# Sliding-window attention in front of a mixture of experts: exponentials by block and head, with the maximum as bias and the row sum as second output

## Chip, cores and metric

One core of one Trainium2 chip runs the whole program. The metric is the time of the device from start to end in microseconds (us), as the median of several executions. Its engines are named as in the profile: PE (matrix multiplication), PEld (PE's weight loads), DVE (the vector engine), ACT (the scalar engine), POOL (GpSimd) and SP (which issues most DMAs).

## The reference

Four batches of 768 tokens, eight heads of 64. Each token attends to the last 128 tokens and to the first four ("sinks"). The result, 3072 rows of 512, goes through a layer of eight experts, of which each token takes two. Of the attention:

```python
scores = scale * np.matmul(q, k.transpose(0, 1, 3, 2))
keep = is_sink | in_window
scores = np.where(keep, scores, -1000000000.0)
scores = scores - np.max(scores, axis=-1, keepdims=True)
a = np.exp(scores)
a = a / (np.sum(a, axis=-1, keepdims=True) + 1e-09)
return np.matmul(a, v).astype(np.float32)
```

The experts follow (noisy gate, best two of eight, two matrix products with a ReLU between, weighted sum). Everything is float32; q and k are scaled so that the scores spread widely.

## The kernel before, in words

**Stages.** The program has an attention stage and an expert stage. In the attention stage the routing of each finished batch is mixed in; the routing of the last batch falls into the expert stage. The change touches the attention stage alone.

**Tiles.** A unit of work `n` (48 in all) is one pair of heads and two neighbouring blocks of 128 queries: four pairs of block and head, `u` = 0 to 3. For each `u` there are 128 rows with `KW` = 132 columns: four for the sinks and 128 for one key per distance. Since a query of a block sees a triangle of its own block and the opposite triangle of the block before, the two triangles fit together into 128 columns. The tile `C(n)` is thus 128 x 4 x 132, in a ring of five (`cbuf`).

**The steps of one unit**, with engine and line: `qk` (PE, L314) makes scores of the previous and the own block in PSUM tile `S`; `prev` (ACT, L317) copies the previous block's with the sinks into `C`; `cur` (DVE, L322 or L324) writes the own block's triangle over it; `cur1` (DVE, L331) masks a few sink columns of a pair of heads' first unit; `mins` (DVE, L334) takes the maximum of each row and `u`, four numbers `mn`; `sub` (POOL, L337, which the profile shows as L221, the line of the helper `minus`) subtracts it; `exps` (ACT, L341) is one exponential over 528 columns with the scale 1/8; `sums` (DVE, L344) adds up each row and `u` over 133 columns, of which the last always holds 1e-9; `sums_i` (DVE, L352) takes the reciprocal. `pcopy` (ACT L363 or POOL L361) and `plow` (POOL, L221 again) split the sink columns into a high and a low part in `pcbuf`. `ptr` (PE, L372) transposes the 128 columns of each `u` into PSUM tile `P`, `ptr_c` (ACT, L375) copies it to `CT`, `ptr_m` (POOL L384 or DVE L382) masks it into `CM`; `pv` (PE, L389 to L398) multiplies by the values and by the differences `dv` of neighbouring value blocks; `sink_c` (ACT, L402), `sinks` (PE, L407), `pv_c` (ACT, L415), `rows` (PE, L420) and `rows_c` (DVE, L423, times the reciprocal) finish the unit, and `rows_d` (SP) writes it out. The line numbers of the changed kernel are one higher from L345 on.

**What sets the order.** Every step is given to a planner (`Plan.op`) with its engine, a booked duration, a priority and the buffers it reads and writes. `Plan.run` walks through time with these durations, takes on each engine the ready step with the lowest priority number, and then emits the instructions in the order of the planned starts. Each engine runs its instructions in exactly that order. The priorities are the unit's number plus a constant from the table `PR` (`exps`, `exps_0` for the first two pairs of heads, `exps_9` for the last two, and so on); `pc_pool` says for how many units in eight `pcopy` goes to POOL. Rings bound how far a unit can run ahead: five of `C`, three of `mn`, four of `sm`, two of `S`, one of `P`, three of `X` (the results in PSUM).

Of the kernel before, what the change touches and what calls it, by code (L numbers as in the profile page):

```python
# [9 lines left out]
F32 = mybir.dt.float32  # L10
# [6 lines left out]
AF = mybir.ActivationFunctionType  # L17
OP = mybir.AluOpType
AX = mybir.AxisListType
BIG = 1.0e30  # L20
PR = dict(dv_pool=3, cm_pool=11, gap=1.5, pc_pool=2, warm=1, cur=0.024, cur1=1.512, cur1_0=-2.463, cur1_9=-0.944,
          cur_0=-2.879, cur_9=7.138, dv=-0.208, dv_0=3.364, dv_9=-0.999, exps=-275.071, exps_0=0.236, exps_9=-12.521,
          ga=217.688, gt=32.64, lg=-2.337, load_qk=1.266, load_v=-14.107, mins=31.945,
          mins_0=-4.24, mins_9=-2.207, nosink=-1.301, nosink_0=-0.047, nosink_9=-0.253, pcopy=6.03, pcopy_0=1.686,
          pcopy_9=7.368, plow=13.607, plow_0=0.131, plow_9=0.771, prev=0.291, prev_0=1.379, prev_9=51.746, ptr=0.719,
          ptr_0=-28.087, ptr_9=2.286, ptr_c=0.721, ptr_c_0=-1.706, ptr_c_9=0.124, ptr_m=1.76, ptr_m_0=1.659,
          ptr_m_9=-7.049, pv=5.174, pv_0=-10.632, pv_9=-9.441, pv_c=0.422, pv_c_0=-1035.731, pv_c_9=-0.357,
          qk=-18.348, qk_0=-9.938, qk_9=1.363, rows=3.058, rows_0=-0.428, rows_9=0.074, rows_c=-3.885,
          rows_c_0=-741.395, rows_c_9=2.644, rt=3.336, sink_c=-35.588, sink_c_0=7.46, sink_c_9=-0.144, sinks=-3.864,
          sinks_0=-0.51, sinks_9=-0.67, sub=15.081, sub_0=14.492, sub_9=19.966, sums=560.828, sums_0=1.201,  # L30
          sums_9=14.127, sums_i=27.946, sums_i_0=-7.208, sums_i_9=-17.917, w1=19.111,
          stay=49.741)
CAP = 832
COLD = 6.0
KQ, PB, XB = 3, 1, 3
FIRST = 4
ZEROS = 16

# [5 lines left out]
class Plan:  # L44
# [16 lines left out]
    def get(self, tag, i, shape=None, dt=F32, pool="sb", pad=None):  # L61
        kx = (tag, i)
        if kx not in self.live:
            more = {"padded_shape": pad} if pad else {}
            self.live[kx] = self.pools[pool].tile(shape, dt, name=tag, bufs=self.rings[tag], **more)
        return self.live[kx]
# [153 lines left out]
def minus(eng, out, a, b):  # L220
    eng.tensor_tensor(out, a, b, op=OP.subtract)  # L221


def attention(tc, plan, consts, cst, sh, qk_t, v, vsink, xbuf):
    nc = tc.nc
    H, S, D, NB, NS, XW = sh.H, sh.S, sh.D, sh.NB, sh.NS, sh.XW
    HP = H // 2
    NJ = NB // 2
    KW = 128 + NS
    NP = sh.B * HP  # L230
    plan.rings.update(vr=2, vn=2, dv=2, skn=2, sqn=2, kq=KQ, C=5, mn=3, sm=4, ri=2, pc=3,
                      CT=2, CM=2, ps=3, xr=3, S=2, P=PB, X=XB, xtn=5, lt=1, lm=1, lg=2)
    get, op = plan.get, plan.op
    jp, idf, idr = cst["jp"], cst["idf"], cst["idr"]
# [7 lines left out]
    nc.vector.tensor_copy(m1, m0[:, :NS])  # L242
    nc.vector.memset(m0[:, :NS], 0.0)

    cbuf = consts.tile([128, plan.rings["C"], 4, KW + 1], F32, name="cbuf")
    nc.gpsimd.memset(cbuf[:, :, :, KW:], 1e-9)

    pcbuf = consts.tile([128, plan.rings["pc"], 128], F32R, name="pcbuf")
    nc.gpsimd.memset(pcbuf.bitcast(F32), 0.0)
# [5 lines left out]
    vst = [plan.next("st") for _ in range(sh.B)]  # L255

    def C(n):
        return cbuf[:, n % plan.rings["C"], :, :KW]

    def vs(b):  # L260
        return get("st", vst[b], [128, 1024], F32, "early").rearrange("p (a g h d) -> p a g h d", a=2, h=2, d=D)
# [71 lines left out]
    def mins(n):  # L333
        nc.vector.tensor_reduce(get("mn", n, [128, 4]), C(n), op=OP.max, axis=AX.X)  # L334

    def sub(n, eng):
        minus(nc.gpsimd if eng == "Pool" else nc.vector, C(n), C(n),  # L337
              get("mn", n)[:, :, None].to_broadcast([128, 4, KW]))

    def exps(n):  # L340
        nc.scalar.activation(C(n), C(n), AF.Exp, scale=1.0 / math.sqrt(D))  # L341

    def sums(n):
        nc.vector.tensor_reduce(get("sm", n, [128, 4]), cbuf[:, n % plan.rings["C"]], op=OP.add, axis=AX.X)  # L344

    def rib(n):
        g, jj = divmod(n, NJ)
# [85 lines left out]
    def P(g, nm):  # L433
        return PR.get(nm, 0) + (PR.get(nm + "_0", 0) if g < 2 else PR.get(nm + "_9", 0) if g >= NP - 2 else 0)

# [6 lines left out]
    def loads_v(g):  # L442
        plan.dma((g - 1) * NJ + PR.get("load_v", 1), lambda: load_v(g), 1.9, w=[("vn", g)])

# [7 lines left out]
    for g in range(NP):  # L452
        p0 = g * NJ
        e = p0 - NJ
        if g:
            load(g, None, (g - 3) * NJ + PR.get("load_qk", 0) if g > 1 else -1980)
            loads_v(g)
        else:
            plan.dma(-1998, lambda: load_v(0), 1.9, w=[("vn", 0)])
        if g % HP == 0:  # L460
            b, z = g // HP, (g - HP) * NJ if g else -6
            plan.dma(z if g else -1996, lambda b=b: sink_values(b), 2.2, w=[("st", vst[b])])
            z += 9 if g else 0
            op("ACT", .95, z, lambda b=b: sink_hi(b), r=[("st", vst[b])], w=[("vr", b)])
            op("DVE", 1.2, z, lambda b=b: sink_lo(b), r=[("st", vst[b])], w=[("vr", b)])
        de = "Pool" if g % 4 < PR.get("dv_pool", 4) else "DVE"
        op(de, 1.5 if de == "Pool" else .74, p0 + .5 + P(g, "dv"), lambda g=g, de=de: dv(g, de), r=[("vn", g)], w=[("dv", g)])
        for jj in range(NJ):
            n = p0 + jj
            if not jj:  # L470
                op("Pool", .05, n + P(g, "nosink"), lambda n=n: nosink(n), w=[("C", n, 0)], u=[("C", n)])
            for a in range(2):
                z = n + .2 * a
                s = 2 * n + a
                need = {max(jj - 1, 0), jj} if not a else {jj}
                op("PE", .5 if jj or a else .3, z + P(g, "qk"), lambda n=n, a=a: qk(n, a),
                   r=[("kq", g, i) for i in sorted(need)], w=[("S", s)], u=[("kq", g)], kind=1)
                if jj or a:
                    op("ACT", .27, z + P(g, "prev"), lambda n=n, a=a: prev(n, a), r=[("S", s)], w=[("C", n, a)], u=[("C", n)])
                op("DVE", .335, z + P(g, "cur"), lambda n=n, a=a: cur(n, a), r=[("S", s)], w=[("C", n, a)], u=[("C", n)])  # L480
            if not jj:
                op("DVE", .085, n + .4 + P(g, "cur1"), lambda n=n: cur1(n), w=[("C", n, 1)], u=[("C", n)])
            op("DVE", .62, n + .4 + P(g, "mins"), lambda n=n: mins(n), r=[("C", n, 0), ("C", n, 1)], w=[("mn", n)], u=[("C", n)])
            op("Pool", 1.03, n + .4 + P(g, "sub"), lambda n=n: sub(n, "Pool"), r=[("mn", n)], w=[("C", n)])
            op("ACT", .53, n + .4 + P(g, "exps"), lambda n=n: exps(n), w=[("C", n)])
            pe = "Pool" if n % 8 < PR.get("pc_pool", 0) else "ACT"
            op(pe, .12 if pe == "ACT" else .23, n + .5 + P(g, "pcopy"), lambda n=n, pe=pe: pcopy(n, pe), r=[("C", n)], w=[("pc", n)])
            op("Pool", .18, n + .5 + P(g, "plow"), lambda n=n: plow(n), r=[("C", n)], w=[("pc", n)])
            op("DVE", .62, n + .8 + P(g, "sums"), lambda n=n: sums(n), r=[("C", n)], w=[("sm", n)])
            op("DVE", .094, n + .6 + P(g, "sums_i"), lambda n=n: sums_i(n), r=[("sm", n)], w=[("rin", n)], u=[("ri", g // HP)])  # L490
            op("PE", .43, n + .5 + P(g, "ptr"), lambda n=n: ptr(n), r=[("C", n)], w=[("P", n + NJ)])
            op("ACT", .48, n + .5 + P(g, "ptr_c"), lambda n=n: ptr_c(n), r=[("P", n + NJ)], w=[("CT", n)])
            me = "Pool" if n % 12 < PR.get("cm_pool", 0) else "DVE"
            op(me, (.6 if jj else .33) * (1 if me == "DVE" else .98), n + .5 + P(g, "ptr_m"), lambda n=n, me=me: ptr_m(n, me),
               r=[("P", n + NJ) if me == "DVE" else ("CT", n)], w=[("CM", n)])
            XA[n] = xa = plan.next("X")
            op("PE", 1.12 if jj else .9, n + .6 + P(g, "pv"), lambda n=n: pv(n),
               r=[("vn", g), ("CT", n), ("dv", g), ("CM", n), ("pc", n)], w=[("X", xa)], kind=2)
            op("ACT", .17, n + .6 + P(g, "sink_c"), lambda n=n: sink_c(n), r=[("X", xa)], w=[("ps", n)])
            op("PE", .24, n + .6 + P(g, "sinks"), lambda n=n: sinks(n), r=[("ps", n), ("vr", g // HP)], w=[("X", xa)], kind=3)  # L500
            op("ACT", .27, n + .6 + P(g, "pv_c"), lambda n=n: pv_c(n), r=[("X", xa)], w=[("xt", n)], u=[("xtn", g)])
            op("PE", .22, n + .7 + P(g, "rows"), lambda n=n: rows(n), r=[("xt", n)], w=[("X", xa)], u=[("xtn", g)])
            op("DVE", .34, n + .7 + P(g, "rows_c"), lambda n=n: rows_c(n), r=[("X", xa), ("rin", n)], w=[("xr", n)],
               u=[("ri", g // HP)])
            plan.dma(n + .7, lambda n=n: rows_d(n), .37, r=[("xr", n)], w=[("xrow", n)])
            yield n
# [770 lines left out]
```

## Time and profile before

| | |
|---|---|
| median of 3 executions | 819.08 us (818.0 to 819.09) |
| the profiled execution | 817.08 us, with a span of 815.5 us from the first to the last instruction |
| busy in the span | PE 777.9 us, PEld 651.9, DVE 437.1, ACT 320.6, POOL 428.2 |
| attention stage | about 8 to 195 us |
| expert stage | about 195 to 815 us |
| mean granted PE clock | 0.985 |

A row of the windows view gives the stretch, its length, then busy time and number of instructions of PE, PEld, DVE, ACT and POOL, the granted PE clock, the share of the DMA engines and GB/s; with a source line it counts that line's instructions alone. A row of the groups view names line, engine, operation, output and input with their shapes and the count; behind the bar stand the busy time and the mean time of one in ns, then the idle time of the engine before them and what ended it. A row of the timeline has start, length, engine, line and operation, and in brackets the idle time before it. A row of the source view has the count and the shortest, median and longest time in ns.

### The profile page before, as it was taken

Reading aid. Unit: us, or ns where it says so; the run is one execution under the profiler, and the core shown is the slowest. Engines: PE = TensorE matmul, PEld = TensorE weight load, DVE = VectorE, ACT = ScalarE, POOL = GpSimd, SP = SyncE. Lnnn points to the kernel's source line nnn. Section 1 sums busy time; section 2 is a strip of 40 time slices with the busy share of each in tenths; the row PEclk is TensorE's granted clock in tenths of the full one; section 3 lists DMA queues with packets and bytes.
Section 4 is the critical chain, followed back from the end, with each engine's and each line's share of the span. In section 5 each row is a group of like instructions: output and inputs, shape, how many; then the busy total and the mean of one; then the engine's idle time right before and its main releaser. Section 6 shows DMA issues by size and latency. Waiting matters only on the chain.

```text
span 815.5 us, 12512 instructions
## 1 busy us (share of the span) xinstructions
PE 777.9 (95%) x4609; PEld 651.9 (80%) x4609; DVE 437.1 (54%) x1086; ACT 320.6 (39%) x641; POOL 428.2 (53%) x544
## 2 busy tenths in 40 slices
PE   7998998988997999999999999999999999999996
PEld 4766766656775888889888988988898889889884
DVE  6899999895543353444346335424543543444220
ACT  4775784754213341333334233323423342333210
POOL 6667777874063444717462753647174445607202
PEclk9999998999998999999999999999999999999999
DMA  7655865536341972545255444616353552534113
GB/s 282 186 167 171 226 219 165 178 96 199 90 122 26 218 177 47 126 129 105 37 142 143 80 82 128 132 40 154 110 106 65 134 136 57 119 109 74 24 24 46
DMA packets 59184, 99.28 MB, mean 122 GB/s; under 512 B 19408, under 2 KB 31952, under 8 KB 59120
## 3 DMA queue, kind: packets, MB, share of 16 engines
q1 hardware_dynamic: 45184, 70.19, 27.8%
q0 software_dynamic: 13936, 28.27, 20.2%
q8 instruction: 37, 0.61, 0.3%
q14 instruction: 27, 0.22, 0.1%
HBM read 69.71 MB, written 28.72 MB: 121 GB/s over the span
## 4 chain that ended last, share of the span: by engine, by line
PE 70%; issue 7%; DVE 7%; POOL 6%; DMA 4%; ACT 3%; another core or an unknown queue 1%; SPq 1%; POOLq 0%; DVEq 0%; ACTq 0%
PE H L971 10%; PE H L973 10%; PE H L972 10%; PE Y L1000 9%; PE Y L1002 9%; PE Y L1001 9%; PE S L314 3%; PE X L395 2%; PE P L372 2%; POOL out L1024 2%; PE Y L1005 1%; PE Y L1006 1%; POOL cbuf L221 1%; POOL xg L824 1%; PE X L398 1%
## 5 line engine op out<-in xcount | busy, mean ns | idle before, releaser
L1024 POOL DMA_INDIRECT out<-y,idx x56 | 91.9, 1642 | 243.3 <-ACT y L1009 227.1
L824 POOL DMA_INDIRECT xg<-x_rows,rt_idq x182 | 181.5, 997 | 55.5 <-issue 54.6
L989 DVE SCALAR_TENSOR_TENSOR h<-H,h 128x384 fp32r<-128x384 f32 (+2 forms) x192 | 79.5, 442 | 222.2 <-ACT h L982 134.5
L973 PE MATMUL H<-skn,w 128*128 128x448 f32 (+3 forms) x512 | 180.6, 353 | 1.7 <-issue 1.7
L971 PE MATMUL H<-skn,w 128*128 128x448 f32 (+3 forms) x512 | 181.4, 354 | 0.0
L972 PE MATMUL H<-sqn,w 128*128 128x448 f32 (+3 forms) x512 | 180.1, 352 | 0.0
L982 ACT ACTIVATE h<-H 128x448 fp32r<-128x448 f32 (+3 forms) x128 | 66.2, 517 | 276.7 <-PE H L973 171.7
L971 PEld LDWEIGHTS H<-skn,w 128*128 128x128 f32 x512 | 96.6, 189 | 9.7 <-issue 1.1
L972 PEld LDWEIGHTS H<-sqn,w 128*128 128x128 f32 x512 | 96.6, 189 | 9.0
L973 PEld LDWEIGHTS H<-skn,w 128*128 128x128 f32 x512 | 96.4, 188 | 5.7 <-issue 0.3
L1000 PE MATMUL Y<-w2b,h 128*128 128x512 f32 x192 | 77.7, 405 | 5.0 <-issue 3.8
L1002 PE MATMUL Y<-w2b,h 128*128 128x512 f32 x192 | 76.8, 400 | 0.5 <-DVE h L989 0.5
L1001 PE MATMUL Y<-w2b,h 128*128 128x512 f32 x192 | 76.6, 399 | 0.0
L1000 PE MATMUL Y<-w2a,h 128*128 128x512 f32 x192 | 75.8, 395 | 0.0
L1001 PE MATMUL Y<-w2a,h 128*128 128x512 f32 x192 | 75.0, 391 | 0.0
L1002 PE MATMUL Y<-w2a,h 128*128 128x512 f32 x192 | 75.0, 390 | 0.0
L314 PE MATMUL S<-kq 64*128 64x264 f32 (+1 forms) x384 | 59.9, 424 | 12.6 <-DVE cbuf L324 6.8
L221 POOL TENSOR_TENSOR cbuf<-cbuf,mn 128x528 f32<-128x528 f32 x48 | 51.9, 1082 | 15.2 <-DVE mn L334 7.6
L314 PEld LDWEIGHTS S<-kq 64*128 64x128 f32 x384 | 33.9, 199 | 27.7 <-DVE cbuf L324 10.0
L881 ACT ACTIVATE skn<-xtn 128x512 fp32r<-128x512 f32 (+1 forms) x49 | 29.5, 602 | 66.9 <-DVE xtn L872 44.4
L1000 PEld LDWEIGHTS Y<-w2b,h 128*128 128x128 f32 x192 | 36.6, 191 | 14.0 <-issue 5.8
L1002 PEld LDWEIGHTS Y<-w2b,h 128*128 128x128 f32 x192 | 36.6, 191 | 10.6 <-DVE h L989 2.1
(183 smaller groups left out, 1254.9 us busy)
## 6 DMA issues: line engine op xcount, KB each, us to landing
st<-in_w1c SPq DMA_DIRECT2D x32, 512.0 KB, 4.4
st<-in_w2c SPq DMA_DIRECT2D x32, 512.0 KB, 3.6
kq<-in_qk_t SPq DMA_DIRECT2D x15, 792.0 KB, 5.7
out<-zt SPq DMA_DIRECT2D x31, 256.0 KB, 4.3
vn<-in_v SPq DMA_DIRECT2D x16, 384.0 KB, 4.0
x_rows<-xr SPq DMA_DIRECT2D x48, 128.0 KB, 3.9
xg<-x_rows,rt_idq POOLq DMA_INDIRECT x182
st<-in_vsink SPq DMA_DIRECT2D x4, 512.0 KB, 4.0
```

What stands on the lines that cost most here:

```text
L221: eng.tensor_tensor(out, a, b, op=OP.subtract)
L314: nc.tensor.matmul(p[:, :2 if j else 1], kq(g)[r, j // 2, 2 + j % 2, NS:], x[:, :2 if j else 1], start=True, stop=True)
L824: nc.gpsimd.indirect_dma_start(out=x[:, i, :], out_offset=None, in_=xbuf.rearrange("r (q d) -> (r q) d", d=sh.SW), in_offset=bass.Indirect ...
L971: nc.tensor.matmul(p, w[:, 0, i], xh, start=(i == 0), stop=False)
L972: nc.tensor.matmul(p, w[:, 0, i], xl, start=False, stop=False)
L973: nc.tensor.matmul(p, w[:, 1, i], xh, start=False, stop=(i == DC - 1))
L982: nc.scalar.activation(get("h", FC * q + f, [128, 2 * 128 * FIRST], F32R)[:, :width], get("H", FC * q + f), AF.Relu)
L989: nc.vector.scalar_tensor_tensor(h[:, o:o + s1 - s0], p[:, s0:s1], 0.0, h[:, s0:s1].bitcast(F32), op0=OP.max, op1=OP.subtract)
L1000: nc.tensor.matmul(p, hh, w[:, 0], start=(f == 0), stop=False)
L1001: nc.tensor.matmul(p, hh, w[:, 1], start=False, stop=False)
L1002: nc.tensor.matmul(p, hl, w[:, 0], start=False, stop=(f == FC - 1))
L1024: d = nc.gpsimd.indirect_dma_start(out=out, out_offset=bass.IndirectOffsetOnAxis(ap=c["idx"][:size(e, t), e, t:t + 1], axis=0), in_=get("y ...
```

## The change

The maximum is no longer subtracted by POOL. Instead, POOL multiplies the four maxima by -1/8 into a new small tile `nb` (ring of three), and ACT runs four exponentials of 132 columns, one for each `u`, each with its column of `nb` as the bias. Each also gives the sum of its row as a second output, into its column of `sm`. The sum pass of DVE and the column of 1e-9 in `cbuf` are gone; POOL adds 1e-9 to `sm` with a small instruction. The planner books 0.9 us for the four exponentials (0.53 for the one before), and 0.1 for each of the two small POOL steps. The table of priorities has new numbers throughout, and `pc_pool` goes from 2 to 4, so that 24 of the 48 `pcopy` are on POOL and 24 on ACT (12 and 36 before).

```diff
-PR = dict(dv_pool=3, cm_pool=11, gap=1.5, pc_pool=2, warm=1, cur=0.024, cur1=1.512, cur1_0=-2.463, cur1_9=-0.944,
...
+PR = dict(dv_pool=3, cm_pool=11, gap=1.5, pc_pool=4, warm=1, cur=-18.937, cur1=29.165, cur1_0=-5.704, cur1_9=11.983,
...
+EXPS = .9
...
+    SCALE = 1.0 / math.sqrt(D)
...
-    cbuf = consts.tile([128, plan.rings["C"], 4, KW + 1], F32, name="cbuf")
-    nc.gpsimd.memset(cbuf[:, :, :, KW:], 1e-9)
+    cbuf = consts.tile([128, plan.rings["C"], 4, KW], F32, name="cbuf")
...
-    def sub(n, eng):
-        minus(nc.gpsimd if eng == "Pool" else nc.vector, C(n), C(n),
-              get("mn", n)[:, :, None].to_broadcast([128, 4, KW]))
+    def bias(n):
+        nc.gpsimd.tensor_scalar(get("nb", n, [128, 4]), get("mn", n), -SCALE, None, op0=OP.mult)

     def exps(n):
-        nc.scalar.activation(C(n), C(n), AF.Exp, scale=1.0 / math.sqrt(D))
+        for u in range(4):
+            nc.scalar.activation(C(n)[:, u, :], C(n)[:, u, :], AF.Exp, bias=get("nb", n)[:, u:u + 1], scale=SCALE,
+                                 accum_out=get("sm", n, [128, 4])[:, u:u + 1])

     def sums(n):
-        nc.vector.tensor_reduce(get("sm", n, [128, 4]), cbuf[:, n % plan.rings["C"]], op=OP.add, axis=AX.X)
+        nc.gpsimd.tensor_scalar(get("sm", n), get("sm", n), 1e-9, None, op0=OP.add)
...
-            op("Pool", 1.03, n + .4 + P(g, "sub"), lambda n=n: sub(n, "Pool"), r=[("mn", n)], w=[("C", n)])
-            op("ACT", .53, n + .4 + P(g, "exps"), lambda n=n: exps(n), w=[("C", n)])
+            op("Pool", .1, n + .4 + P(g, "sub"), lambda n=n: bias(n), r=[("mn", n)], w=[("nb", n)])
+            op("ACT", EXPS, n + .4 + P(g, "exps"), lambda n=n: exps(n), r=[("nb", n)], w=[("C", n), ("sm", n)])
...
-            op("DVE", .62, n + .8 + P(g, "sums"), lambda n=n: sums(n), r=[("C", n)], w=[("sm", n)])
+            op("Pool", .1, n + .8 + P(g, "sums"), lambda n=n: sums(n), w=[("sm", n)])
```

What the engines then hold in a row, at three places. First ACT in the first third of the attention stage, before (`ps` is the sink part's copy, `CT` the transposed weights, `xtn` the result, `cbuf<-S` the copy of scores):

```order
L415 ACTIVATE xtn<-X 128x256
L363 ACTIVATE pcbuf<-cbuf 128x8x4
L375 ACTIVATE CT<-P 128x512
L317 ACTIVATE cbuf<-S 128x2x132 x2
L341 ACTIVATE cbuf<-cbuf 128x4x132
L317 ACTIVATE cbuf<-S 128x2x132
L341 ACTIVATE cbuf<-cbuf 128x4x132
L402 ACTIVATE ps<-X 128x128
```

And now, at the same depth:

```order
L416 ACTIVATE xtn<-X 128x256
L341 ACTIVATE cbuf,sm<-cbuf,nb 128x132 x4
L317 ACTIVATE cbuf<-S 128x264 x2
L403 ACTIVATE ps<-X 128x128
L376 ACTIVATE CT<-P 128x512
L341 ACTIVATE cbuf,sm<-cbuf,nb 128x132 x4
L416 ACTIVATE xtn<-X 128x256
L364 ACTIVATE pcbuf<-cbuf 128x8x4
```

One instruction for a unit has become four that follow each other, with the copies of PSUM tiles behind them as before; the copy into `pcbuf` is there for every second unit.

Second, POOL at about the same place, before (`cbuf<-cbuf,mn` is the subtraction, `pcbuf<-cbuf,pcbuf` the low part, `dv` the differences of values):

```order
L221 TENSOR_TENSOR cbuf<-cbuf,mn 128x4x132
L384 AFFINE_SELECT CM<-CT 128x512
L361 CAST pcbuf<-cbuf 128x8x4
L221 TENSOR_TENSOR cbuf<-cbuf,mn 128x4x132
L221 TENSOR_TENSOR pcbuf<-cbuf,pcbuf 128x8x4
L221 TENSOR_TENSOR cbuf<-cbuf,mn 128x4x132
L384 AFFINE_SELECT CM<-CT 128x256
```

And now:

```order
L345 TENSOR_SCALAR sm<-sm 128x4
L221 TENSOR_TENSOR pcbuf<-cbuf,pcbuf 128x8x4
L385 AFFINE_SELECT CM<-CT 128x512
L337 TENSOR_SCALAR nb<-mn 128x4
L345 TENSOR_SCALAR sm<-sm 128x4
L221 TENSOR_TENSOR dv<-vn 128x640
L221 TENSOR_TENSOR pcbuf<-cbuf,pcbuf 128x8x4
```

In the place of each subtraction stands the bias step, and one more small step a unit adds the 1e-9.

Third, DVE where the first batch's routing begins (`rt_` tiles), before:

```order
L334 TENSOR_REDUCE mn<-cbuf 128x4
L344 TENSOR_REDUCE sm<-cbuf 128x4
L352 RECIPROCAL ri<-sm 128x2x2
L324 COPY_PREDICATED cbuf<-le,S 128x2x128
L334 TENSOR_REDUCE mn<-cbuf 128x4
L662 SCALAR_TENSOR_TENSOR rt_c<-lg,rt_c 128x48
L344 TENSOR_REDUCE sm<-cbuf 128x4
L663 TENSOR_TENSOR rt_ln<-rt_ln,rt_c 128x48
```

And now:

```order
L324 COPY_PREDICATED cbuf<-le,S 128x2x128
L334 TENSOR_REDUCE mn<-cbuf 128x4
L324 COPY_PREDICATED cbuf<-le,S 128x2x128
L424 TENSOR_TENSOR xr<-X,ri 128x256
L663 SCALAR_TENSOR_TENSOR rt_c<-lg,rt_c 128x48
L424 TENSOR_TENSOR xr<-X,ri 128x256
L664 TENSOR_TENSOR rt_ln<-rt_ln,rt_c 128x48
```

The sum passes are gone from the row, and the results (`xr`) have moved up between the steps of the routing.

More of the change, by code (lines that the diff above doesn't have):

```diff
@@ L20 @@
 BIG = 1.0e30
-PR = dict(dv_pool=3, cm_pool=11, gap=1.5, pc_pool=2, warm=1, cur=0.024, cur1=1.512, cur1_0=-2.463, cur1_9=-0.944,
[L22 to L32, printed above, removed]
@@ new lines @@
+PR = dict(dv_pool=3, cm_pool=11, gap=1.5, pc_pool=4, warm=1, cur=-18.937, cur1=29.165, cur1_0=-5.704, cur1_9=11.983,
+          cur_0=6.512, cur_9=-0.33, dv=-52.458, dv_0=0.577, dv_9=0.531, exps=3.096, exps_0=-0.226, exps_9=1.099,
+          ga=217.688, gt=-3.723, lg=0.386, load_qk=-0.97, load_v=12.837, mins=6.316, mins_0=-0.113, mins_9=0.34,
+          nosink=0.838, nosink_0=-1.615, nosink_9=-32.443, pcopy=-13.774, pcopy_0=-6.332, pcopy_9=7.568, plow=-0.057,
+          plow_0=-0.114, plow_9=-9.657, prev=1.89, prev_0=0.072, prev_9=-17.32, ptr=0.719, ptr_0=-56.204,
+          ptr_9=-1.387, ptr_c=-0.414, ptr_c_0=0.17, ptr_c_9=-0.397, ptr_m=-0.055, ptr_m_0=0.45, ptr_m_9=5.503,
+          pv=5.174, pv_0=-2.533, pv_9=12.038, pv_c=-19.622, pv_c_0=0.367, pv_c_9=1.329, qk=-5.586, qk_0=-6.302,
+          qk_9=0.62, rows=-1.013, rows_0=-0.373, rows_9=-19.786, rows_c=0.7, rows_c_0=7.677, rows_c_9=-0.247,
+          rt=4.365, sink_c=1.261, sink_c_0=-666.238, sink_c_9=-2.991, sinks=-24.385, sinks_0=-0.138, sinks_9=-34.12,
+          sub=15.911, sub_0=0.295, sub_9=1.973, sums=167.455, sums_0=-77.997, sums_9=0.86, sums_i=1.253,
+          sums_i_0=17.481, sums_i_9=1.58, w1=22.319, stay=49.268)
@@ L229, in attention @@
     KW = 128 + NS
+    SCALE = 1.0 / math.sqrt(D)
     NP = sh.B * HP
-    plan.rings.update(vr=2, vn=2, dv=2, skn=2, sqn=2, kq=KQ, C=5, mn=3, sm=4, ri=2, pc=3,
+    plan.rings.update(vr=2, vn=2, dv=2, skn=2, sqn=2, kq=KQ, C=5, mn=3, nb=3, sm=4, ri=2, pc=3,
                       CT=2, CM=2, ps=3, xr=3, S=2, P=PB, X=XB, xtn=5, lt=1, lm=1, lg=2)
@@ L257, in C @@
     def C(n):
-        return cbuf[:, n % plan.rings["C"], :, :KW]
+        return cbuf[:, n % plan.rings["C"]]
     def vs(b):
```

## Prediction

> **What bounds the kernel now.** The windows view first, because the change touches only the attention stage. Each row gives start and end, length, then busy us and instruction count of PE, PE's weight loads, DVE, ACT and POOL; the last row is what follows the stage.
>
> ```profile
> 8.00:60.00 52.00, 50.95 (x458) 36.96 (x459) 44.05 (x104) 37.81 (x101) 34.74 (x58) 1.00 0.63 208
> 60.00:78.00 18.00, 15.93 (x155) 10.94 (x154) 17.86 (x57) 12.31 (x35) 13.61 (x22) 1.00 0.64 193
> 78.00:104.00 26.00, 25.84 (x259) 18.96 (x260) 25.08 (x66) 17.32 (x45) 18.08 (x31) 0.94 0.69 189
> 104.00:131.00 27.00, 22.27 (x204) 16.08 (x204) 25.94 (x69) 16.96 (x47) 19.93 (x29) 0.90 0.58 181
> 131.00:157.00 26.00, 25.34 (x260) 18.98 (x262) 23.77 (x59) 19.09 (x49) 23.63 (x32) 0.97 0.80 238
> 157.00:181.00 24.00, 19.33 (x195) 13.45 (x191) 23.89 (x72) 12.99 (x38) 19.26 (x34) 1.00 0.31 75
> 8.00:195.00 187.00, 172.80 (x1672) 125.85 (x1672) 170.34 (x447) 124.55 (x334) 140.88 (x221) 0.97 0.61 183
> 195.00:815.00 620.00, 602.83 (x2930) 525.05 (x2929) 262.31 (x619) 193.90 (x306) 283.27 (x305) 0.99 0.44 102
> ```
>
> The stage lasts 187 us, and two kinds of stretch alternate in it. In 8 to 60, 78 to 104 and 131 to 157 PE is busy 97 to 99% of the time. In 60 to 78, 104 to 131 and 157 to 181, where the routing of a finished batch is mixed in, DVE is busy 96 to 99% and PE falls to 81 to 88%. At the rate of 78 to 104 (259 instructions in 26 us) the stage's 1672 PE instructions need 168 us: 19 us of the 187 are PE waiting, and that is all that a change off PE can win. ACT has a third of the stage free. After 195 us PE is busy 97%, on the experts, whose code is unchanged; I carry the stage's gain or loss into the span one to one.
>
> The chain of waits for 8 to 195 us is cut at the window's edge by the width of the line; what is needed stands in it.
>
> ```profile
> by line: PE S L314 14.9%; PE X L395 8.4%; PE P L372 7.5%; POOL cbuf L221 6.0%; PE X L398 5.1%; issue 4.0%; PE X L420 3.6%; PE X L407 3.3%; DVE mn L334 3.2%; DMA kq<-in_qk_t 3.2%; DVE cbuf L324 3.1%; ACT cbuf L341 3.0%; DVE sm L344 2.7%; PE
> ```
>
> Of 187 us, the subtraction on POOL carries 6.0% (11.2 us), the exponential 3.0% (5.6 us) and the sum pass 2.7% (5.0 us): 21.8 us of the chain are the three steps that the change rewrites. Here are their groups (line, engine, shapes, count, then busy us and mean ns).
>
> ```profile
> L341 ACT ACTIVATE cbuf<-cbuf 128x528 f32<-128x528 f32 x48 | 30.9, 645 | 15.1 <-POOL cbuf L221 14.2 <-POOL cbuf L327 0.6
> L363 ACT ACTIVATE pcbuf<-cbuf 128x32 fp32r<-128x32 f32 x36 | 7.8, 230 | 0.0
> L344 DVE TENSOR_REDUCE sm<-cbuf 128x4 f32<-128x532 f32 x48 | 33.1, 696 | 4.3 <-ACT cbuf L341 4.1
> L221 POOL TENSOR_TENSOR cbuf<-cbuf,mn 128x528 f32<-128x528 f32 x48 | 51.9, 1082 | 15.2 <-DVE mn L334 7.6 <-ACT ps L402 2.8 <-ACT CT L375 2.5
> L763 POOL TENSOR_SCALAR em<-vm 128x4 f32<-128x4 f32 x1 | 0.2, 198 | 0.0
> L361 POOL CAST pcbuf<-cbuf 128x32 fp32r<-128x32 f32 x12 | 3.7, 316 | 2.0 <-ACT cbuf L341 2.0
> ```
>
> **The change, part by part.** *DVE* loses 48 sum passes, 33.1 us. In the DVE-bound stretches that is time won; in the others DVE was not last.
>
> *POOL* loses 48 subtractions (51.9 us). It gains 48 bias steps and 48 additions of 1e-9, 128x4 each. The nearest row is the single 128x4 TENSOR_SCALAR at 198 ns, so 96 x 0.2 = 19 us, and 12 more of the small copies (24 for 12) at 316 ns, 3.8 us. POOL falls from 141 to about 112 us of 187 and bounds nothing.
>
> *ACT* loses 48 exponentials of 528 columns and 12 small copies, and gains 192 exponentials of 132 columns that take the bias from a column of SBUF and also give a row sum. Their price is the term on which all hangs, and before has no such instruction. Call E the time for which one group of four keeps ACT. Width: from 230 ns at 32 columns to 645 at 528 is 0.837 ns a column, so 314 ns at 132. Operand from a column: the next fence has the scaled copy of the experts (scale from a column) beside a plain copy of the same shape, both out of PSUM: 688 against 595, so 93 ns more, 407. Overlap: its rows of start and length follow, then plain ones.
>
> ```profile
> L1009 ACT ACTIVATE y<-Y,wc 128x512 f32<-128x512 f32 x48 | 32.0, 688 | 17.3 <-PE Y L1002 10.3 <-PEq L1111 4.8
> L375 ACT ACTIVATE CT<-P 128x512 f32<-128x512 f32 x48 | 28.6, 595 | 3.5 <-PE P L372 2.8 <-DVE CM L382 0.2
> 442.17 1.27 ACT L1009 ACTIVATE y<-Y,wc 128x512 f32<-128x512 f32 x2
> 41.61 0.65 ACT L341 ACTIVATE cbuf<-cbuf 128x528 f32<-128x528 f32 x1 [0.20 <-POOL cbuf L221]
> 42.16 0.58 ACT L375 ACTIVATE CT<-P 128x512 f32<-128x512 f32 x1
> 75.54 0.21 ACT L701 ACTIVATE z<-z 128x6 f32<-128x6 f32 x1 [1.06 <-POOL z L700]
> 75.65 0.65 ACT L317 ACTIVATE cbuf<-S 128x264 f32<-128x264 f32 x2
> ```
>
> Two scaled copies take 1.27, not 1.38, and the exponential at 41.61 lets the next start after 0.55 of its 0.645: neighbours overlap by about 0.10. So 0.30 us each without the row sum, E = 1.2 where it was 0.55. The row sum: no row shows one. From below it costs nothing (nothing in the trace suggests a gain); from above, getting each sum out is a small ACT instruction of its own. The smallest in the trace is 128x6: 0.21 long, and the next starts 0.11 after it. With 0.11 each, E = 1.6; with 0.21, E = 2.0; with 0.21 and no overlap on either side, 4 x (0.407 + 0.21) = 2.45. I take the middle of the two nearest ways, 0.16, so E = 1.83, and keep 1.2 to 2.45 as the ends.
>
> The Trainium skill (ScalarE: Activation LUTs, What ACT_TABLE_LOAD costs) prices an ACTIVATE with a bias from a column at 280 ns plus 0.833 ns a column, with 93 ns of overlap: an estimate of 0.297 each and 1.19 the group. It gives no price for the row sum. The trace agrees on the operand (93 ns, above).
>
> *What E does to the PE-bound stretches.* The exponentials in them (busy and count) are:
>
> ```profile
> 8.00:60.00 52.00, 10.98 (x17) 1.00 0.63 208
> 78.00:104.00 26.00, 4.51 (x7) 0.94 0.69 189
> 131.00:157.00 26.00, 5.08 (x8) 0.97 0.80 238
> ```
>
> ACT without them, plus 1.83 for each: 37.81 - 10.98 + 17 x 1.83 = 57.9 in a stretch of 52; 17.32 - 4.51 + 12.8 = 25.6 in 26; 19.09 - 5.08 + 14.6 = 28.7 in 26. The overruns, 5.9 + 2.7, make 8.6; 12 small copies fewer at about 0.12 take off 1.4 at most, of which I count 1 here. So ACT adds about 7.6 us. What is queued behind: each ACT instruction after a group is a copy of scores, a copy of transposed weights or a copy of results, and PE needs their PSUM buffers (two of scores, one of transposes). Who waits is PE. The group itself now waits for the bias on POOL in place of the subtraction, and behind that wait stand the same copies.
>
> *The chain.* 21.8 us go. About 10 subtractions on it (11.2 / 1.08) become bias steps of 0.2: 2.1. About 9 exponentials (5.6 / 0.645) become groups of 1.83: 16.5. Seven sum passes (5.0 / 0.696) become small POOL steps: 1.4, nothing if hidden. Net -1.8.
>
> *DVE beside POOL.* One small DVE operation shows what POOL's work costs it:
>
> ```profile
> L331 DVE TENSOR_TENSOR cbuf<-cbuf,m x16: 144/462/1606, 6.4 to 172.9; 128x8 f32<-128x8 f32 x16
> L331 DVE TENSOR_TENSOR cbuf<-cbuf,m 128x8 f32<-128x8 f32 x15 | 8.1, 537 | 0.1
> ```
>
> Eight columns take 144 ns at best and up to 1606, which is longer than a whole subtraction; 15 x (537 - 144) = 5.9 us are waiting. With 52 us of POOL's 141 gone I count half of it as won: -3. If nothing is won this term is 0. The Trainium skill (SBUF — State Buffer, Who interferes with whom) says that a DVE instruction with two SBUF inputs and a POOL instruction that reads SBUF lock each other out; the spread of this row agrees.
>
> *Sum:* +7.6 - 1.8 - 3 = about +3 us (part of the chain's longer groups lies inside the overruns; I leave that uncorrected, since an engine in order at full load also loses time that I don't count). PE's own count of instructions is the same, and the new order moves its groups by a place or two; I cost that at nothing, since DVE and POOL have slack to hide it, and if ACT is full the order cannot.
>
> The profiled execution took 817.08 us, its span of 815.5 and 1.6 around it; the runs' median is 819.08, 2.0 above. The sum moves both: 820 profiled, 822 as a median.
>
> **The rivals.** *A, the row sum is free* (E 1.2 to 1.4). At 1.2 the three stretches need 47.2 of 52, 21.2 of 26 and 23.6 of 26, so ACT adds nothing; the chain gains 21.8 - 2.1 - 1.4 - 10.8 = 7.5, DVE 3: 819 - 10.5 = 808.5. For it: nothing in before shows a second instruction. The page of the skill, taken alone, is this rival. Against it: a sum of a row that ACT has to write elsewhere is something that none of its other instructions does. *B, a cheap row sum* (E 1.4 to 1.7). At 1.63: overruns of 2.5 and 1.1, less 1; chain -3.6; DVE -3: 815. *C* is my forecast (E 1.7 to 2.1). *D, each sum is read with the engine emptied before and after* (E above 2.1). At 2.45: overruns 16.5, 4.0, 7.6 and, in 60 to 78 with its four groups, about 1.5, less 1: 28.6; chain 22.1 + 2.1 + 1.4 - 21.8 = +3.8; DVE -3: 848. It is the same mechanism as C with a worse price; the point from which ACT decides against the change is E = 1.75. That the change does not do what it says can be left out: no sum pass over the block stands on DVE in the new order.
>
> **How the numbers follow.** Chances: A 0.25, B 0.20, C 0.35, D 0.20. C is the likeliest and gives 822; its own range, E 1.7 to 2.1, is about 817 to 832. The range for all: A's lowest 10% of chance below 808 and D's upper 10% above 840 are left out. A difference of 0.2%, 1.6 us, is about what a measurement of this kernel tells from none. Faster by more: A and about two thirds of B, 0.38; within: the rest of B and C's lowest part, 0.12; slower by more: 0.50, most of C and all of D.
>
> **What would show it.** In the changed profile: ACT exponentials of 128x132 with a mean near 407 ns, and a second small instruction behind each, or none; group start to group start of about 1.83 where four follow each other; ACT busy in the stage up from 125 to about 180 us; DVE down by 33 or more, with the eight-column addition nearer 0.3; POOL near 112; PE waiting for ACT in 8 to 60. Rows of 0.41 with the next start 0.30 later and nothing between make A right and me wrong; PE as full as before in the first 60 us with ACT below 90% does so as well.

## The result and the profile after

The changed kernel takes 838.51 us (median of 4 runs, 835.37 to 839.23) where the kernel before takes 819.09: 19.4 us more, a ratio of 1.0233 with a 95% interval of 1.0206 to 1.0260. The forecast said slower with a chance of 0.5, 822 us as the likeliest value and 808 to 840 as the range. The sign came, and 838.51 lies near the upper edge of the range; the loss was over six times the forecast's 3 us.

All of it lies in the attention stage. The first product of the first expert, in the source view of that line before and after (its second number pair is the first and last start):

```profile
L971 PE MATMUL H<-skn,w x512: 307/350/797, 201.1 to 786.5; 128*128 128x448 f32 x75, 128*128 128x384 f32 x74, 128*128 128x512 f32 x11, 128*128 128x320 f32 x11
```

```profile
L972 PE MATMUL H<-skn,w x512: 302/350/792, 222.6 to 808.5; 128*128 128x448 f32 x75, 128*128 128x384 f32 x74, 128*128 128x512 f32 x11, 128*128 128x320 f32 x11
```

It starts at 201.1 us before and at 222.6 after. From there to the end it is 815.5 - 201.1 = 614.4 us before and 837.4 - 222.6 = 614.8 after. The loss was carried one to one.

Now what a group of exponentials costs, in the timeline of ACT after (start, length, instruction):

```profile
40.39 0.41 ACT L341 ACTIVATE cbuf<-cbuf,nb 128x132 f32<-128x132 f32 x1
40.70 0.19 ACT L341 ACTIVATION_READ_ACCUMULATOR cbuf<-cbuf,nb 128x1 f32 x1
40.79 0.39 ACT L341 ACTIVATE cbuf<-cbuf,nb 128x132 f32<-128x132 f32 x1
41.09 0.19 ACT L341 ACTIVATION_READ_ACCUMULATOR cbuf<-cbuf,nb 128x1 f32 x1
...
41.86 0.19 ACT L341 ACTIVATION_READ_ACCUMULATOR cbuf<-cbuf,nb 128x1 f32 x1
41.96 0.57 ACT L376 ACTIVATE CT<-P 128x512 f32<-128x512 f32 x1
```

Each exponential is followed by an instruction of its own that reads the sum out. From the first start to that of the next other instruction, 40.39 to 41.96, the group keeps ACT 1.57 us: 0.30 for each exponential and 0.09 for each reading. The groups view has them over the stage, with POOL's two new steps, DVE's eight-column addition and the wait of DVE's reciprocal:

```profile
L341 ACT ACTIVATE cbuf<-cbuf,nb 128x132 f32<-128x132 f32 x192 | 75.1, 396 | 16.3 <-POOL nb L337 16.1
L341 ACT ACTIVATION_READ_ACCUMULATOR cbuf<-cbuf,nb 128x1 f32 x192 | 36.7, 191 | 0.0
L337 POOL TENSOR_SCALAR nb<-mn 128x4 f32<-128x4 f32 x47 | 12.3, 262 | 18.6 <-DVE mn L334 15.0 <-PE X L408 2.3 <-DVE ri L353 0.9
L345 POOL TENSOR_SCALAR sm<-sm 128x4 f32<-128x4 f32 x48 | 11.0, 230 | 33.5 <-ACT cbuf L341 31.8
L331 DVE TENSOR_TENSOR cbuf<-cbuf,m 128x8 f32<-128x8 f32 x15 | 4.1, 274 | 0.2
L353 DVE RECIPROCAL ri<-sm 128x4 f32<-128x4 f32 x48 | 8.2, 174 | 33.8 <-POOL sm L345 33.8
```

And the windows view, in some of the same stretches as in the prediction (a unit now ends later, so the stretches hold other work), and for the stage up to its new end:

```profile
8.00:60.00 52.00, 44.64 (x345) 29.69 (x346) 27.98 (x68) 41.89 (x171) 22.01 (x64) 0.97 0.56 184
78.00:104.00 26.00, 21.99 (x216) 15.88 (x217) 21.25 (x76) 19.76 (x85) 14.67 (x42) 1.00 0.60 170
131.00:157.00 26.00, 21.83 (x214) 16.57 (x212) 23.61 (x70) 19.85 (x78) 19.09 (x39) 0.93 0.64 171
8.00:217.00 209.00, 182.61 (x1673) 130.80 (x1673) 137.33 (x400) 165.30 (x658) 116.75 (x280) 0.96 0.55 167
```

In 8 to 60 us PE gets 345 instructions through where it had 458, and is busy 44.6 us of 52. No other engine is full: ACT 41.9, DVE 28.0, POOL 22.0. Over the stage ACT is busy 165 of 209 us, 79%. The slack is spread over all engines, and each waits for another. PE's busy time in the stage grew as well, from 172.8 to 182.6 us for the same instructions, so of the stage's 22 us about 12 are idle time of PE and 10 lie in what counts as busy. In the groups view, 9.0 of the 10 are in the three groups whose waits for ACT grow below: L372 (now L373) from 31.1 to 34.3 us, L407 (L408) from 17.8 to 20.6, L420 (L421) from 17.4 to 20.4. Why they count as busy for longer was not taken apart.

The chain of waits for 8 to 215 us shows where the time goes round:

```profile
by line: ACT cbuf L341 29.0%; PE S L314 8.1%; PE X L396 6.1%; PE P L373 6.0%; ACT CT L376 4.1%; PE X L399 3.7%; ACT cbuf L317 3.7%; PE X L421 3.2%; ACT xtn L416 3.0%; issue 2.9%; DVE cbuf L324 2.6%; PE X L408 2.2%; DVE mn L334 1.9%; POOL nb
```

The exponentials are 29% of it, 60 us, where the subtraction, the exponential and the sum pass together were 21.8. PE's own waits, before and after (us in total, times, longest):

```profile
PE S L314 <- DVE cbuf L324: 6.8, 5, 3.0
PE X L407 <- ACT ps L402: 1.7, 3, 0.7
PE P L372 <- ACT CT L375: 0.8, 3, 0.4
```

```profile
PE X L421 <- ACT xtn L416: 7.9, 11, 1.3
PE X L408 <- ACT ps L403: 7.6, 9, 2.2
PE P L373 <- ACT CT L376: 3.8, 4, 1.5
PE S L314 <- DVE cbuf L324: 3.3, 5, 1.2
PE P L373 <- ACT cbuf L341: 3.0, 1, 3.0
```

Before, PE stood 2.5 us in these rows for ACT; now 22.3. Of the 22.3, 15.5 are waits for `xtn` and `ps`, which PE's next matrix product reads; 3.8 are for the copy `CT`, which frees the only PSUM tile `P`; 3.0 are for an exponential itself. One of these waits in the two timelines after:

```profile
50.14 0.61 PE L399 MATMUL X<-CM,dv 128*64 128x128 f32 x8
...
50.96 0.60 PE L373 MATMUL P<-idf,cbuf 128*128 128x128 f32 x4
52.87 0.44 PE L408 MATMUL X<-ps,vr 128*128 128x128 f32 x2 [1.31 <-ACT ps L403]
```

```profile
51.01 0.40 ACT L341 ACTIVATE cbuf<-cbuf,nb 128x132 f32<-128x132 f32 x1
...
52.17 0.40 ACT L341 ACTIVATE cbuf<-cbuf,nb 128x132 f32<-128x132 f32 x1
52.47 0.19 ACT L341 ACTIVATION_READ_ACCUMULATOR cbuf<-cbuf,nb 128x1 f32 x1
52.56 0.26 ACT L403 ACTIVATE ps<-X 128x128 fp32r<-128x128 f32 x1
```

PE stands still for 1.31 us for the small copy `ps`, 0.26 us long. The products whose end the copy waits for (L399) are over at 50.75, but on ACT a group of exponentials has its place ahead of the copy and holds it from 51.01 to 52.56.

### The profile page after: what moved, and what is told of

It is laid out like the page before. It is cut to its first block, busy times and chain, and to the rows that moved or that the text cites. A ratio compares the mean times of both kernels' runs of the same rounds, so it can differ in the third digit from the quotient of the medians.

```text
span 837.4 us, 12817 instructions
## 1 busy us (share of the span) xinstructions
PE 787.1 (94%) x4609; PEld 656.4 (78%) x4609; DVE 403.6 (48%) x1038; ACT 360.8 (43%) x965; POOL 405.5 (48%) x603
## 3 DMA queue, kind: packets, MB, share of 16 engines
q0 software_dynamic: 13936, 28.27, 19.4%
## 4 chain that ended last, share of the span: by engine, by line
PE 71%; ACT 12%; issue 6%; DVE 5%; POOL 3%; DMA 1%; another core or an unknown queue 1%; SPq 0%; POOLq 0%; DVEq 0%; ACTq 0%
PE H L974 10%; PE H L972 10%; PE H L973 10%; PE Y L1001 9%; PE Y L1003 9%; PE Y L1002 9%; ACT cbuf L341 7%; PE S L314 2%; PE X L396 2%; PE Y L1007 2%; PE Y L1006 2%; PE P L373 1%; POOL out L1025 1%; ACT CT L376 1%; PE X L399 1%
## 5 line engine op out<-in xcount | busy, mean ns | idle before, releaser
L341 ACT ACTIVATE cbuf<-cbuf,nb 128x132 f32<-128x132 f32 x192 | 75.1, 396 | 16.3 <-POOL nb L337 16.1
L314 PEld LDWEIGHTS S<-kq 64*128 64x128 f32 x384 | 33.8, 200 | 16.2 <-DVE cbuf L324 6.6
```

Source lines behind the costliest of these rows:

```text
L314: nc.tensor.matmul(p[:, :2 if j else 1], kq(g)[r, j // 2, 2 + j % 2, NS:], x[:, :2 if j else 1], start=True, stop=True)
L341: nc.scalar.activation(C(n)[:, u, :], C(n)[:, u, :], AF.Exp, bias=get("nb", n)[:, u:u + 1], scale=SCALE, accum_out=get("sm", n, [128, 4])[ ...
```

## The experiments

Theory Q: the loss comes from the order. Every engine runs a list that the planner wrote with 0.9 us for a group that takes 1.57, and the copies behind each group come late for PE. Rivals: C, ACT's added work is the limit in whatever order; T, the new table of priorities is bad in itself; and later W, DVE's wait in front of the reciprocal. The runs were made in three sets (e1 to e4, e5 to e8, e9 to e12), each on one chip together with the kernel before. Its medians there were 815.9, 806.7 and 808.2 us, so what counts is the ratio to it. The change itself was measured apart from the three sets.

| run | ratio to before | 95% interval |
|---|---|---|
| the change | 1.0233 | 1.0206 to 1.0260 |
| e1_book157 | 1.0067 | 1.0039 to 1.0096 |
| e2_old_table | 1.0351 | 1.0315 to 1.0387 |
| e3_table_alone | 1.0036 | 1.0014 to 1.0058 |
| e4_no_sum | 1.0019 | 0.9999 to 1.0038 |
| e5_one_exp | 0.9841 | 0.9806 to 0.9875 |
| e6_direct | 1.0266 | 1.0229 to 1.0302 |
| e7_retuned | 1.0011 | 0.9991 to 1.0031 |
| e8_retuned_no_add | 0.9946 | 0.9921 to 0.9971 |
| e9_third | 1.0019 | 1.0001 to 1.0038 |
| e10_half | 0.9967 | 0.9958 to 0.9977 |
| e11_two_thirds | 0.9948 | 0.9932 to 0.9965 |
| e12_book09_again | 1.0245 | 1.0226 to 1.0264 |

**The booking alone.**

```diff
-EXPS = .9
+EXPS = 1.57
```

> The changed kernel with one number altered: the planner books 1.57 us, which a group of four exponentials takes in the trace, where it booked 0.9. Theory Q (the order was written for 0.9, and engines that run in order wait for each other where ACT is late): 820 to 830 us, with PE waiting less. Theory C (ACT's added work itself is the limit, in whatever order): 835 to 842, no change worth the name. Theory T (the new table of priorities is bad in itself): 835 to 842 too, since the table stays.

821.66 us beside 815.86: of the 2.33% of loss 1.66 are gone, with the same instructions, the same table and the same work on every engine. Only the lists differ. The windows view of its first stretch, and PE's waits for ACT:

```profile
8.00:60.00 52.00, 46.64 (x391) 32.32 (x392) 30.11 (x74) 41.91 (x169) 22.86 (x65) 1.00 0.56 192
```

```profile
PE X L421 <- ACT xtn L416: 3.9, 4, 1.4
PE P L373 <- ACT CT L376: 2.4, 4, 1.2
PE X L408 <- ACT ps L403: 0.6, 1, 0.6
```

With ACT busy 41.9 us in both, PE gets 391 instructions through instead of 345, and its waits for these three copies fall from 19.3 to 6.9 us. C and T had said no change; the measured time lies in Q's range.

**The tables, each way.** The changed code with the old table, and the old code with the new table:

```diff
-PR = dict(dv_pool=3, cm_pool=11, gap=1.5, pc_pool=4, warm=1, cur=-18.937, ...
+PR = dict(dv_pool=3, cm_pool=11, gap=1.5, pc_pool=2, warm=1, cur=0.024, ...
```

> The changed kernel's code with the table of priorities of the kernel before. Theory T: back to 812 to 822. Theory Q: the planner still books 0.9, so the order misses the chip in the same way, 832 to 845. Theory C: 835 to 842.

> The kernel before with the changed kernel's table of priorities alone (pc_pool 4 among it), and none of the new code. Theory T: 829 to 840, most of the loss. Theories Q and C: within 5 us of 819, since the bookings of the old code fit the chip.

The old table with the new code is worse than the new one, 1.0351 (it also moves 12 small copies back to ACT, by `pc_pool`), and the new table on the old code costs 0.36%. T falls: the table is not the cause.

**The change's own order, with a shorter group.** First without the second output, so that nothing is read back; the kernel leaves out the row sums:

```diff
-            nc.scalar.activation(C(n)[:, u, :], ..., bias=get("nb", n)[:, u:u + 1], scale=SCALE,
-                                 accum_out=get("sm", n, [128, 4])[:, u:u + 1])
+            nc.scalar.activation(C(n)[:, u, :], ..., bias=get("nb", n)[:, u:u + 1], scale=SCALE)
...
-        nc.gpsimd.tensor_scalar(get("sm", n), get("sm", n), 1e-9, None, op0=OP.add)
+        nc.gpsimd.tensor_scalar(get("sm", n, [128, 4]), C(n)[:, :, 131], 50.0, None, op0=OP.add)
```

> The changed kernel in its own order, without the second output of the exponentials, so that nothing reads a row sum back; the small POOL step behind them adds 50 to one column of the block instead, so that it still waits for the exponentials and the waits stay the same. What is left out: the row sums. A group then keeps ACT about 1.2 us instead of 1.57. Theory C: 48 x 0.37 = 18 us of ACT, of which 12 to 18 come back: 820 to 826. Theory Q: most of the loss comes from where the groups stand; 3 to 9 us come back: 829 to 835.

817.23 us, 1.0019: 2.14% or 17.5 us come back for about 48 x 0.37 = 18 us less of ACT. That is the gain that C forecast; Q's, 3 to 9 us, was too small. In this order each us that a group takes between 1.2 and 1.57 delays the end by about as much. C's reason, a full ACT, does not hold here: in the change's own run ACT was busy 79% of the stage.

Then, against the run just shown, one exponential of 528 columns in the place of the four; this leaves out the bias too, so ACT no longer waits for POOL's step `nb` (16.1 us of idle time in the changed kernel):

```diff
-        for u in range(4):
-            nc.scalar.activation(C(n)[:, u, :], C(n)[:, u, :], AF.Exp, bias=get("nb", n)[:, u:u + 1], scale=SCALE)
+        nc.scalar.activation(C(n), C(n), AF.Exp, scale=SCALE)
```

> The changed kernel in its own order, with one exponential of 528 columns and no bias in place of the four; the small POOL step behind it adds 50 to one column, as in the run without the second output. Left out: the maximum as bias and the row sums. A group keeps ACT 0.55 us. The first theory of capacity (C) has ACT below PE already at 1.2 us, so from 1.2 to 0.55 nothing or little more: 811 to 818. The theory that time hangs on ACT's place in the order (Q) gives a smaller gain for each us than from 1.57 to 1.2, where 17.8 us of ACT gave 21: between 3 and 12 us more, 805 to 814.

0.9841, which would be 803 us beside the 815.9 of the first set: a little below Q's range and well below C's. From 1.2 us to 0.55 a group, 31 us less of ACT bring 1.8%, 14 us. So the price of an ACT microsecond in this order is about 1.0 us of the end from 1.57 to 1.2, and at most 0.5 below, with whatever the wait for the bias was worth in it. What PE can do without the old DVE and POOL work is seen here too, in the first stretch:

```profile
8.00:60.00 52.00, 51.52 (x462) 36.24 (x462) 38.14 (x93) 38.23 (x97) 26.11 (x78) 1.00 0.68 226
```

**DVE's 33.8 us in front of the reciprocal.** The largest wait of the changed kernel; POOL's step keeps its place, but the reciprocal no longer reads it:

```diff
-        nc.gpsimd.tensor_scalar(get("sm", n), get("sm", n), 1e-9, None, op0=OP.add)
+        nc.gpsimd.tensor_scalar(get("sn", n, [128, 4]), get("sm", n), 1e-9, None, op0=OP.add)
```

> The changed kernel in its own order; POOL's addition of 1e-9 goes to a tile that nobody reads, and the reciprocal takes the sum that ACT wrote. Left out: the 1e-9, which no sum of one or more shows in float32. In the trace of the changed kernel DVE stands 33.8 us in front of the reciprocal, waiting for this POOL step. If that wait was a cause (theory W): 8 to 15 us faster, 823 to 831. If it is only where DVE spends time that it has (Q and C): within 4 us of 838.

1.0266, not to be told from the change's 1.0233. W falls. Of the 33.8 us of wait, 23.1 are left, now straight for ACT, and the end did not come earlier:

```profile
DVE ri L353 <- ACT cbuf L341: 23.1, 20, 2.6
```

The longest wait in the list was idle time of an engine that had some to spare.

**The right booking with a table made for it.** The planner alone, run on random changes of the priorities, gave a table with a shorter planned end for the booking of 1.57:

```diff
-PR = dict(dv_pool=3, cm_pool=11, gap=1.5, pc_pool=4, warm=1, cur=-18.937, ...
+PR = dict(dv_pool=3, cm_pool=11, gap=1.5, pc_pool=4, warm=1, cur=-70.491, ...
...
-EXPS = .9
+EXPS = 1.57
```

Then the new way without POOL's addition, with `pc_pool` at 2 and a table of its own. This kernel is built on the kernel before, with the new way switched on for all 48 units (`ACC`) and POOL's bias step booked at 0.15:

```diff
-PR = dict(dv_pool=3, cm_pool=11, gap=1.5, pc_pool=2, warm=1, cur=0.024, ...
+PR = dict(dv_pool=3, cm_pool=11, gap=1.5, pc_pool=2, warm=1, cur=-16.65, ...
...
+EXPS, BIAS = 1.57, .15
+ACC = frozenset([0, 1, 2, ..., 47])
...
-            op("DVE", .62, n + .8 + P(g, "sums"), lambda n=n: sums(n), r=[("C", n)], w=[("sm", n)])
+            if n not in ACC:
+                op("DVE", .62, n + .8 + P(g, "sums"), lambda n=n: sums(n), r=[("C", n)], w=[("sm", n)])
```

> The changed kernel with the booking of 1.57 us and a table of priorities searched anew for that booking. The run with the booking alone took 821.7. Q: better again by 3 to 10 us, 811 to 819, near the kernel before. C: no better than 821.

> As the run before it, but without POOL's addition of 1e-9 (the reciprocal reads what ACT wrote), with pc_pool 2 and a table searched for that. Q: 2 to 6 us below the run with the step, 808 to 815. C: the same as it, since ACT's work is the same or a little more.

1.0011 and 0.9946. With the right order the change is level with the kernel before, and without the addition half a per cent faster than it. Which difference makes the second better than the first (the addition, `pc_pool`, the bias step's booking, the other search) was not taken apart; in the change's own order the addition as an input of the reciprocal cost nothing. The first stretch of the faster one:

```profile
8.00:60.00 52.00, 49.67 (x447) 35.85 (x448) 33.75 (x86) 49.36 (x209) 20.36 (x56) 1.00 0.64 213
```

Here ACT is busy 49.4 of 52 us and PE gets 447 instructions through. ACT could have been this full in the changed kernel and was not. From 28 to 58 us both ACT and PE are busy without a gap:

```profile
28.00:58.00 30.00, 30.00 (x296) 22.45 (x293) 19.50 (x52) 30.00 (x137) 12.93 (x34) 1.00 0.66 206
```

So C's limit exists, but only behind the limit that the order set: once the list fits, ACT's work fills this stretch.

**The same booking error once more.** The faster kernel with its booking set back:

```diff
-EXPS, BIAS = 1.57, .15
+EXPS, BIAS = .9, .15
```

> The fastest kernel so far (all units the new way, no addition on POOL, searched table, 0.9946 of before) with its booking set from 1.57 back to 0.9, and nothing else. Q: the order is again written for a group that is too short, so 1 to 2% are lost: ratio 1.004 to 1.015. C: ACT's work is the same, so the ratio stays at 0.992 to 0.998.

1.0245: 3.0% are lost by one number in the planner, more than Q said, with ACT's work unchanged. The table had been made for a booking of 1.57, so a table that does not suit 0.9 is part of this price. The granted PE clock was 0.98 in the stage of both kernels and does not account for it. Its first stretch has 380 PE instructions instead of 447, and ACT busy 43.7 us instead of 49.4:

```profile
8.00:60.00 52.00, 47.57 (x380) 31.50 (x380) 29.47 (x72) 43.70 (x181) 18.95 (x49) 1.00 0.56 192
```

**Mixes.** The new way for some units only (without the addition, booked at 1.57, tables searched), the old way for the rest:

```diff
+            if n in ACC:
+                op("Pool", BIAS, ..., lambda n=n: bias(n), r=[("mn", n)], w=[("nb", n)])
+                op("ACT", EXPS, ..., lambda n=n: exps4(n), r=[("nb", n)], w=[("C", n), ("sm", n)])
+            else:
+                op("Pool", 1.03, ..., lambda n=n: sub(n, "Pool"), r=[("mn", n)], w=[("C", n)])
+                op("ACT", .53, ..., lambda n=n: exps(n), w=[("C", n)])
```

> Every third unit takes the new way (without POOL's addition of 1e-9, booked at 1.57), the others the old way with the subtraction, one exponential and the sum pass; table searched for it. Q: with the order right, ACT's added 16 us and DVE's saved 11 fit into slack; ratio to the kernel before 0.985 to 0.997. If the new way gains nothing by itself once the order is right: 0.998 to 1.004.

> Every second unit takes the new way, as in the run with a third. Q: ratio 0.985 to 0.997, the best of the mixes if ACT and DVE end up evenly filled. If the new way gains nothing by itself: 0.998 to 1.004.

> Two of three units take the new way. Q: between the half and the run with all units (0.9946): 0.988 to 0.996. If ACT's work alone counts: slower than the half by 8 x 1.0 us, 1%.

1.0019, 0.9967 and 0.9948: with a third of the units the new way gains nothing, with half of them 0.3%, with two thirds 0.5%. Q's forecast for the third failed and those for the half and the two thirds held only at their slower ends; none is better than all units the new way (0.9946). The fastest kernels found beat both given ones, the one before by about 0.5%.

## Why the prediction was right in the sign and wrong in the reason

- **The sign was luck.** The sum came out slower because E was too large; with the measured E it says faster (two points below). The loss came from a term that stood in it at nothing.
- **E, the time of a group: mis-sized, inside its bounds.** 1.83 was forecast, 1.57 measured. The exponential was right (0.407 forecast, 0.396 measured, next start after 0.30). The reading of the sum is the separate instruction that I had supposed, but costs 0.09 where I took 0.16. The price that the Trainium skill (ScalarE: Activation LUTs, What ACT_TABLE_LOAD costs) gives for an operand from a column, 1.19 as an estimate for the group, fits the exponentials (4 x 0.30) and leaves out the 4 x 0.09 of the readings.
- **ACT's overrun of the PE-bound stretches (+7.6): fell.** With E = 1.57 the same sum gives overruns of 26.8 + 17 x 1.57 - 52 = 1.5 and 14.0 + 8 x 1.57 - 26 = 0.6, less 1 for the small copies, the chain -4.2 and DVE -3: about 6 us *faster*, my rival B. The kernel is 19.4 slower. ACT was not full: 41.9 us of 52 in the first stretch. The term itself is not refuted: where the list was made for 1.57, in the fastest kernel, ACT does fill that stretch, and its 0.9946, 4.4 us faster, is near the sum's 6; that kernel also lacks the addition and has a table of its own.
- **The step that failed** is the sentence that PE's new order costs nothing, "since DVE and POOL have slack to hide it, and if ACT is full the order cannot". DVE's and POOL's slack does not help a PE that waits for copies queued on ACT. The booking in the diff, 0.9, stood beside my own E of 1.83, and I did not ask what a list written for 0.9 does when the group takes twice that. The two runs that change the booking alone put it at 1.7% and 3.0%, 14 and 24 us.
- **What is queued behind the groups: half right.** It is the copies that PE waits for. But only 3.8 of the 19.3 us are a wait for a PSUM buffer to be freed (`CT`); 15.5 are waits for data that PE reads next (`xtn` and `ps`). And the price was put on ACT's capacity, not on the copies' lateness.
- **The chain: half right.** The subtraction and the sum pass left it, but the exponentials grew to 60 us of it where I had 16.5. That the late groups drew the chain onto ACT fits this, but no run shows it apart.
- **DVE and POOL: right and harmless.** DVE lost 33.5 us (437.1 to 403.6 in the span). POOL went from 141 to 117 us in the stage where I had 112, as its small steps take 262 and 230 ns, not 200. The eight-column addition fell from 537 to 274 ns. The Trainium skill (SBUF — State Buffer, Who interferes with whom) has a DVE instruction with two SBUF inputs contend with POOL instructions that read SBUF; the fall agrees, with POOL's long subtractions gone. Little of the saved time reached the end: DVE is now idle for 72 of the stage's 209 us, before for 17 of 187.
- **The rivals.** D's place (ACT) and nearly its size came with a price of the group below C's. That B was the right case for E and D nearly for the time shows that E alone was not the quantity that decides.
- **Two slips in the working.** 4 x (0.407 + 0.21) is 2.47, not 2.45, which changes nothing. And the count of PE's instructions is no measure of its work: from 8 to 60 us PE is as busy as from 78 to 104 with 8.8 instructions per us instead of 10.0. By its busy time PE was idle for 14 us of the stage, not 19.

What stays open: why the change's order charges about 1.0 us for each us of ACT above 1.2 and at most half of that below was measured, not explained; why the same matrix products count as busy for longer behind the waits; and how much of the last 0.5% is the search and how much the new way.

## What to carry to other kernels

Where engines run lists that a planner wrote, a changed instruction's booked time is part of the change: measure it and book that before judging the idea. An engine that is busy 80% can still set the end, if what stands behind its long instruction is what another engine waits for; look at the waits of the engine that should be full, not at the longest wait of the list. Whoever splits one instruction into four with a second output each should count the instructions that read that output back.

## What was not expected of the hardware

The second output of an exponential comes out through an instruction of its own, 191 ns in the profile with the next start 0.09 us after it, although the program's list has only the four exponentials. And the kernel before took 819.1, 815.9, 806.7 and 808.2 us as the median of four sets of runs, the last three on three different chips. The medians lie up to 1.5% apart, more than most of the differences here: only ratios within one set could tell these kernels apart.
